# Decode attention beside a gMLP: the output weights of the gMLP laid out on other lanes

## The chip, the cores and the metric

The kernel runs on one core of one Trainium2 chip. A core has a matrix engine (PE, with its weight loads listed as PEld), a vector engine (DVE), a scalar engine (ACT), a general engine (POOL) and a sequencer for transfers (SP). Sixteen DMA engines carry data between the chip's main memory (DRAM) and the on-chip memory (SBUF), which has 128 lanes. The matrix engine writes to a smaller memory (PSUM). The metric is the device time of one execution in microseconds (us), as a median over runs.

## The reference

One decode step for four sequences, D = 640. The input x is normalised once. Attention uses 32 heads of 128 with caches of 4096 positions. A gMLP runs on the same normalised input, and both are added to x.

```python
xn = layernorm(x)                                   # x: 4 x 1 x 640
q = (xn @ wq) as 32 heads of 128                    # wq: 640 x 4096
p = softmax(q . k_cache / sqrt(128))                # caches: 4 x 32 x 4096 x 128
a = (p . v_cache) as 4096 columns @ wo              # wo: 4096 x 640
z = gelu(xn @ w_in)                                 # w_in: 640 x 1728
z1, z2 = z[:, :864], layernorm(z[:, 864:])
b = (z1 * (w_sp * z2 + b_sp)) @ w_out               # w_out: 864 x 640
out = x + a + b
```

All is bf16. The caches are 2 x 134 MB, so nearly all bytes moved are keys and values. w_out is 1.1 MB.

## The kernel before

The attention is cut into 16 tiles (8 heads of one sequence each). Each tile has 8 MB of keys and 8 MB of values, 64 KB to a lane. In the main loop DVE multiplies the keys by the spread query (product, L463), folds halves (fold, L477), PE sums the rest (sums, L489), DVE finishes the scores (row_sums, L500), and ACT takes the exponentials (L556). PE multiplies them with the values (weighted, L582) and the result is gathered (diag, L605) until the projection with wo at the end (group_proj, through add_out, L225).

SBUF has two slots for keys (pool kp) and one for values (pool vp), each 64 KB to a lane. A slot that holds other data is reused when its last reader is done. wq sits in the first key slot, the first keys in the second, and the second keys in the first one again, after wq. w_in and w_out sit together in the value slot (w_sb, L106 to L112), and the first values come after the gMLP has read them.

Work written before the `with tc.manual_schedule` block (L694) is put in order by a scheduler. Inside the block, PE, DVE, ACT and SP follow the order of the code. All large transfers are issued by SP, in one order: w_out's 128 lanes, wq, w_in, the rest of w_out, first keys, second keys, first values, and then keys and values in turn. An issue that has to wait holds up those behind it. The first two calls of load_k (L170, L308) stand before the block.

The gMLP (L331 to L435) multiplies w_in in 70 small matmuls (zT, L331), passes through a chain of short DVE and ACT steps, and ends in y, the gated product. w_out's rows 0 to 767 lie six to a lane on 128 lanes. The other 96 rows lie six to a lane on 16 lanes, filled by four transfers (L128) of four lanes each. Since y comes out of PE with 96 of its entries on 96 lanes, six selecting matmuls with columns of the identity (ye_ps, L423) turn them into 16 lanes of six, ACT copies them (L430), and add_out adds one product per row of a lane: 6 + 6 = 12 calls of four matmuls.

Of the kernel before, what the change touches and what calls it, by code (L numbers as in the profile page):

```python
# [17 lines left out]
def kernel(  # L18
# [14 lines left out]
    nc = tc.nc  # L33
    P = nc.NUM_PARTITIONS
    Bsz, Sq, D = A_x.shape
    _, H, S, Dh = A_k_cache.shape
    HD = A_wq.shape[1]
    F = B_w_in.shape[1]
    Fh = F // 2
    DC = D // P  # L40
# [13 lines left out]
    SLOT = NC * Dh  # L54
# [9 lines left out]
    WJ = WH * Dh // P  # L64
    WW = 2
    WR = NG * ROWS
    NFF = Fh // P
    TL = 16
    TK = (Fh - NFF * P) // TL
    TE = 4  # L70
    NFC = NFF + TK
    F0 = NFF * P
    TF = TL * TK
    NZ = NFF + 1
    assert F0 + TF == Fh and TF <= P
    NQ = 4
    NO = D // NQ
    REP = GW // Bsz
# [15 lines left out]
    def k_slot(name):  # L94
        return kp.tile([P, SLOT], BF16, tag="k", name=name)

    def v_slot(name):
# [7 lines left out]

    w_sb = v_slot("w_sb")  # L106
    w_in_sb = w_sb[:, 0 : DC * F].rearrange("p (c n) -> p c n", c=DC)
    w_out_sb = w_sb[:, DC * F : DC * F + NFC * D].rearrange("p (k n) -> p k n", k=NFC)
    y_at = DC * F + NFC * D
    y_rep = w_sb[:, y_at : y_at + (NZ + TK) * GW].rearrange(  # L110
        "p (k b r) -> p k b r", b=Bsz, r=REP
    )  # L112
    yT, yE = y_rep[:, 0:NZ], y_rep[:TL, NZ : NZ + TK]
    nc.sync.dma_start(
        out=w_out_sb[:, 0:NFF, :], in_=B_w_out[0 : NFF * P].rearrange("(p k) n -> p k n", k=NFF)
    )

    wq_t = k_slot("wq")[:, 0 : DC * HD].rearrange("p (c n) -> p c n", n=HD)
    nc.sync.dma_start(out=wq_t, in_=A_wq.rearrange("(p c) n -> p c n", c=DC))

    wsp_bf = const.tile([1, 1], BF16)
# [4 lines left out]
    nc.sync.dma_start(out=w_in_sb, in_=B_w_in.rearrange("(p c) n -> p c n", c=DC))  # L126
    for l in range(TL // TE):
        nc.sync.dma_start(  # L128
            out=w_out_sb[:TL, NFF:NFC, :].rearrange("(e l) k n -> e l (k n)", e=TE)[:, l],
            in_=B_w_out[F0:Fh].rearrange("(e l k) n -> e l (k n)", e=TE, k=TK)[:, l],  # L130
        )

    def kv_view(cache, i):
# [8 lines left out]
    def load_k(i):  # L142
        t = k_slot("k_nat")
        nc.sync.dma_start(out=t[:], in_=kv_view(A_k_cache, i))
        k_tiles[i] = t[:].rearrange("p (c d) -> p c d", d=Dh)
# [21 lines left out]
            for j0, j1 in zip(WO_CUTS[g], WO_CUTS[g][1:]):  # L167
                nc.sync.dma_start(out=t[:, g, j0:j1, :], in_=wo_v[g][:, j0:j1, :])

    load_k(0)  # L170


    ident = const.tile([P, P], BF16)
    make_identity(nc, ident[:])
    ident_f = const.tile([P, P], FP32)
    nc.gpsimd.tensor_copy(out=ident_f[:], in_=ident[:])
    eps_tile = const.tile([P, 1], FP32)
# [13 lines left out]
    for i in range(NSTAT):  # L191
# [9 lines left out]
        out=xn_bf,  # L201
# [21 lines left out]
    def add_out(lhsT, rhs, start=False, stop=False):  # L223
        for q in range(NQ):
            nc.tensor.matmul(  # L225
                out=out_ps[GW * q : GW * q + lhsT.shape[1], :],
                lhsT=lhsT,
                rhs=rhs[:, q * NO : (q + 1) * NO],
                start=start,
                stop=stop,  # L230
            )
# [73 lines left out]
            in_=qT_ps[:, :, :, :, 0],  # L305
        )

    load_k(1)  # L308


    GM = 2 * NZ * Bsz
    gm = {}
# [10 lines left out]
    def gmlp():  # L323
        zz, gw, gt, gz, sq = (gm[n] for n in ("zz", "gw", "gt", "gz", "sq"))
        zT = ps_pv.tile([P, 2, NZ, Bsz], FP32, tag="pv", name="zT")
        for t in range(2):
            f1 = t * Fh + F0
            w_t = w_in_sb[:, :, t * Fh : f1].rearrange("p c (f k) -> p c k f", k=NFF)
            for k in range(NZ):
                for c in range(DC):  # L330
                    nc.tensor.matmul(  # L331
                        out=zT[: P if k < NFF else TF, t, k, :],
                        lhsT=w_t[:, c, k, :] if k < NFF else w_in_sb[:, c, f1 : f1 + TF],
                        rhs=xnT[:, c, :],
                        start=(c == 0),
                        stop=(c == DC - 1),
                    )
        nc.vector.tensor_copy(out=zz[:, :, 0:NFF, :], in_=zT[:, :, 0:NFF, :])
        nc.vector.tensor_copy(out=zz[:TF, :, NFF:NZ, :], in_=zT[:TF, :, NFF:NZ, :])
        nc.vector.tensor_tensor(out=gw, in0=zz, in1=zz, op=ALU.mult)  # L340
        nc.vector.tensor_scalar(
            out=gw, in0=gw, scalar1=0.044715, scalar2=1.0, op0=ALU.mult, op1=ALU.add
        )
        nc.vector.tensor_tensor(out=gw, in0=gw, in1=zz, op=ALU.mult)
        nc.scalar.activation(
            out=gt, in_=gw, func=ACT.Tanh, scale=math.sqrt(2.0 / math.pi)
        )
        nc.vector.tensor_scalar(
            out=gt, in0=gt, scalar1=1.0, scalar2=0.5, op0=ALU.add, op1=ALU.mult
        )  # L350
        nc.vector.tensor_tensor(out=gz, in0=zz, in1=gt, op=ALU.mult)
        nc.vector.tensor_tensor(out=sq, in0=gz[:, 1, :, :], in1=gz[:, 1, :, :], op=ALU.mult)

        s_ps = ps_m.tile([1, 2, NZ, Bsz], FP32, tag="m", name="ln_ps")
        for n, src in enumerate((gz[:, 1, :, :], sq)):
            nc.tensor.matmul(
                out=s_ps[:, n, :, :], lhsT=ones_col[:], rhs=src, start=True, stop=True
            )
        st, ac = gm["st"], gm["ac"]
        mean_t = st[:, 0:Bsz]  # L360
        ex2_t = st[:, Bsz : 2 * Bsz]
        var_t = st[:, 2 * Bsz : 3 * Bsz]
        rst_t = st[:, 3 * Bsz : 4 * Bsz]
# [27 lines left out]
        nc.vector.tensor_tensor(out=tmp_t, in0=ac[:, 0:Bsz], in1=mean_t, op=ALU.mult)  # L391
        nc.vector.tensor_scalar(
            out=ac[:, Bsz : 2 * Bsz],
            in0=tmp_t,
            scalar1=-1.0,
            scalar2=bsp_t[:, 0:1],
            op0=ALU.mult,
            op1=ALU.add,
        )
        ac_ps = ps_m.tile([P, 2 * Bsz], FP32, tag="m", name="ac_ps")  # L400
        nc.tensor.matmul(
            out=ac_ps[:], lhsT=ones_row[:], rhs=ac[:], start=True, stop=True
        )
        ac_sb = work.tile([P, 2 * Bsz], FP32, name="ac_sb")
        nc.scalar.copy(out=ac_sb[:], in_=ac_ps[:])
        nc.vector.tensor_tensor(
            out=sq,
            in0=gz[:, 1, :, :],
            in1=ac_sb[:, None, 0:Bsz].to_broadcast([P, NZ, Bsz]),
            op=ALU.mult,  # L410
        )
        nc.vector.tensor_tensor(
            out=sq,
            in0=sq,
            in1=ac_sb[:, None, Bsz : 2 * Bsz].to_broadcast([P, NZ, Bsz]),
            op=ALU.add,
        )
        nc.vector.tensor_tensor(
            out=yT[:, :, :, 0], in0=gz[:, 0, :, :], in1=sq, op=ALU.mult
        )  # L420
        ye_ps = ps_m.tile([TL, TK, Bsz], FP32, tag="m", name="ye_ps")
        for k in range(TK):
            nc.tensor.matmul(  # L423
                out=ye_ps[:, k, :],
                lhsT=ident[:TF, :TF].rearrange("p (f k) -> p k f", k=TK)[:, k, :],
                rhs=yT[:TF, NFF, :, 0],
                start=True,
                stop=True,
            )
        nc.scalar.copy(out=yE[:, :, :, 0], in_=ye_ps[:])  # L430
        for k in range(NFC):
            if k < NFF:
                add_out(yT[:, k].rearrange("p b r -> p (b r)"), w_out_sb[:, k, :])
            else:
                add_out(yE[:, k - NFF].rearrange("p b r -> p (b r)"), w_out_sb[:TL, k, :])  # L435


    qbcs, scores, sums_ps, maxes, pms, pvs, es = {}, {}, {}, {}, {}, {}, {}
# [253 lines left out]

    E = mybir.EngineType
    with tc.manual_schedule(engines={E.PE, E.DVE, E.Activation, E.SP}):  # L694
        stage_q(0)
        gmlp()
        load_v(0, v_slot("v_nat"))
# [94 lines left out]
```

## Time and profile before

| | us |
|---|---|
| median of 3 runs | 661.47 |
| lowest and highest run | 661.35, 662.2 |
| the profiled execution | 661.68 |
| its span | 659.8 |
| busy in it: PE, PEld, DVE, ACT, POOL | 293.0, 127.5, 491.7, 35.1, 3.5 |
| granted clock of PE, mean | 0.715 of full |

The profile is of one execution. Its page gives busy time per engine, forty slices of the span, the DMA queues, and the chain of work that ended last. That chain follows each step back to whatever released it. Answers of the trace give the same execution instruction by instruction: start, length, engine, line, tile, and in brackets the idle time before it and what ended that. Times count from the start of the span. The 282.55 MB are moved at a mean of 428 GB/s. On SP, a line names the issue of a transfer and not its duration.

### The profile page before, as it was taken

How to read it: one execution, taken by the hardware profiler on the slowest of the kernel's cores; microseconds unless marked ns; L12 is line 12 of the kernel's file. 1: busy time of each engine (PE TensorE's matmuls, PEld its weight loads, DVE VectorE, ACT ScalarE, POOL GpSimd, SP SyncE). 2: the span in 40 equal slices, each digit the busy share in tenths (PEclk: the TensorE clock that was granted, in tenths of full speed). 3: DMA queues.
4: the chain of work that ended last, by engine and by line, in shares of the span. 5: the costliest groups of instructions: out<-in, count | busy, mean ns of one | idle time of the engine just before them, and what ended most of it. 6: DMA issues, size and time to landing. Idle time of an engine off the chain costs nothing.

```text
span 659.8 us, 4735 instructions
## 1 busy us (share of the span) xinstructions
PE 293.0 (44%) x2099; PEld 127.5 (19%) x2099; DVE 491.7 (75%) x222; ACT 35.1 (5%) x95; POOL 3.5 (1%) x18
## 2 busy tenths in 40 slices
PE   0513453535426163552626344362624516263646
PEld 0301121212112021210202112120311202031223
DVE  1249999959597795959779569986959599695851
ACT  0300000000000000000000000000000000000010
POOL 1000000000000000000000000000000000000000
PEclk9756687876758777675867757787775758768697
DMA  9999999999999999999999999999999999999996
GB/s 378 452 433 445 417 430 438 438 433 442 413 441 438 433 431 445 421 442 425 433 437 438 433 438 421 433 438 437 427 445 421 438 441 422 433 445 430 437 407 279
DMA packets 5700, 282.55 MB, mean 428 GB/s; under 512 B 668, under 2 KB 800, under 8 KB 1072
## 3 DMA queue, kind: packets, MB, share of 16 engines
q1 hardware_dynamic: 5658, 282.24, 98.9%
q8 instruction: 16, 0.26, 0.1%
q14 instruction: 4, 0.03, 0.0%
q10 hardware_dynamic: 22, 0.01, 0.0%
HBM read 282.24 MB, written 0.01 MB: 428 GB/s over the span
## 4 chain that ended last, share of the span: by engine, by line
DMA 49%; DVE 40%; PE 8%; issue 2%; ACT 1%; DVEq 0%; SPq 0%; ACTq 0%
DMA k_nat<-in_A_k_cache_dram 42%; DVE k_nat L463 24%; DVE k_nat L477 12%; DMA v_last<-in_A_v_cache_dram 6%; PE s_ps L489 6%; DVE s_sb L500 3%; PE pv L582 1%; ACT p L556 1%; DMA w_sb<-in_B_w_out_dram 1%; DVE m L509 1%; PE mT L514 0%; DVE nm L519 0%; PE out_ps L225 0%; PE o_ps L605 0%; PE den L622 0%
## 5 line engine op out<-in xcount | busy, mean ns | idle before, releaser
L463 DVE TENSOR_TENSOR k_nat<-k_nat,qbc 128x16384 bf16<-128x16384 bf16 x32 | 278.0, 8688 | 96.5 <-DMA k_nat<-in_A_k_cache_dram 96.5
L489 PE MATMUL s_ps<-k_nat,ident 128*128 128x512 bf16 x528 | 182.5, 523 | 140.3 <-DVE k_nat L477 140.3
L477 DVE TENSOR_TENSOR k_nat<-k_nat 128x8192 bf16<-128x8192 bf16 x31 | 136.7, 4409 | 0.0
L489 PEld LDWEIGHTS <-ident 128*128 128x128 bf16 x528 | 64.6, 128 | 247.6 <-DVE k_nat L477 124.5
L514 PE MATMUL mT<-ident_f,m 128*1 128x128 f32 x16 | 5.8, 360 | 160.0 <-DVE m L509 160.0
L582 PE MATMUL pv<-v_nat,pm 128*32 128x512 bf16 x960 | 56.1, 387 | 0.8 <-DVE pm L567 0.8
L500 DVE TENSOR_REDUCE s_sb<-s_ps 128x128 f32<-128x1024 f32 x32 | 39.0, 1218 | 3.8 <-PE s_ps L489 3.7
L582 PEld LDWEIGHTS <-pm 128*32 128x32 bf16 x1024 | 27.2, 101 | 36.1 <-issue 10.5
L514 PEld LDWEIGHTS mT<-ident_f,m 128*1 128x1 f32 x16 | 1.3, 79 | 167.8 <-DVE m L509 160.6
L567 DVE TENSOR_TENSOR pm<-p,own_c 128x2048 bf16<-128x2048 bf16 x16 | 19.6, 1225 | 15.3 <-ACT p L556 15.3
L556 ACT ACTIVATE p<-s_sb,nb 128x256 bf16<-128x256 f32 x16 | 8.1, 508 | 391.0 <-DVE nb_h L538 391.0
L605 PE MATMUL o_ps<-e,pick 128*32 128x128 f32 x128 | 17.0, 276 | 11.2 <-ACT e L592 11.2
L605 PEld LDWEIGHTS o_ps<-e,pick 128*32 128x32 f32 x128 | 12.7, 109 | 18.7 <-ACT e L592 18.7
L592 ACT COPY e<-pv 128x512 f32<-128x512 f32 x16 | 9.4, 586 | 70.4 <-PE pv L582 61.0
L530 PE MATMUL nb_ps<-nm,ones_row 1*128 1x8 f32 x32 | 9.1, 356 | 6.0 <-DVE nm L519 6.0
L301 DVE COPY qT<-qT_ps 128x64 bf16<-128x64 bf16 x2 | 0.4, 224 | 14.6 <-PE qT_ps L296 14.6
L519 DVE TENSOR_REDUCE nm<-mT 1x8 f32<-1x128 f32 x16 | 4.5, 279 | 7.3 <-PE mT L514 7.3
L530 PEld LDWEIGHTS nb_ps<-nm,ones_row 1*128 1x128 f32 x32 | 7.6, 293 | 10.5 <-DVE nm L519 9.8
L457 ACT CAST qbc<-qbc_ps 128x128 bf16<-128x128 f32 x16 | 4.3, 266 | 92.5 <-PE qbc_ps L449 92.5
L285 PE MATMUL q_ps<-wq,xnT_r 128*32 128x512 bf16 x40 | 3.8, 561 | 10.7 <-DMA wq<-in_A_wq_dram 10.7
L582 PE MATMUL pv<-v_last,pm 128*32 128x512 bf16 x64 | 6.0, 559 | 4.2 <-DMA v_last<-in_A_v_cache_dram 4.2
L622 PE MATMUL den<-ones_col,acc_h 128*32 128x1 f32 x8 | 1.0, 189 | 14.9 <-DVE acc_h L615 14.9
(95 smaller groups left out, 74.6 us busy)
## 6 DMA issues: line engine op xcount, KB each, us to landing
wq<-in_A_wq_dram SPq DMA_DIRECT2D x1, 5120.0 KB, 16.3
wo<-in_A_wo_dram SPq DMA_DIRECT2D x1, 2560.0 KB
w_sb<-in_B_w_in_dram SPq DMA_DIRECT2D x1, 2160.0 KB, 20.9
wo<-in_A_wo_dram SPq DMA_DIRECT2D x1, 1760.0 KB
w_sb<-in_B_w_out_dram SPq DMA_DIRECT2D x1, 960.0 KB
wo<-in_A_wo_dram SPq DMA_DIRECT2D x1, 640.0 KB, 25.0
k_nat<-in_A_k_cache_dram SPq DMA_DIRECT2D x16, 39.6
v_nat<-in_A_v_cache_dram SPq DMA_DIRECT2D x15, 33.3
```

The costliest lines, as they stand in the source:

```text
L463: nc.vector.tensor_tensor(out=part(i, u), in0=part(i, u), in1=qbcs[i][:, None, :].to_broadcast([P, UC, Dh]), op=ALU.mult,)
L477: nc.vector.tensor_tensor(out=t[:, :, 0:HD2], in0=t[:, :, 0:HD2], in1=t[:, :, HD2:Dh], op=ALU.add)
L489: nc.tensor.matmul(out=sums_ps[i][:, c : c + SC], lhsT=ident[:], rhs=t[:, c : c + SC, g * RW : (g + 1) * RW], start=(g == 0), stop=(g == n ...
L500: nc.vector.tensor_reduce(out=scores[i][:, u * UC : (u + 1) * UC], in_=sums_ps[i][:], axis=AX.X, op=ALU.add,)
L509: nc.vector.tensor_reduce(out=m1[:], in_=scores[i][:], axis=AX.X, op=ALU.max)
L514: nc.tensor.transpose(out=mT[:], in_=maxes[i][:], identity=ident_f[:])
L530: nc.tensor.matmul(out=nb_ps[:], lhsT=ones_row[:], rhs=maxes[i][:], start=True, stop=True)
L556: nc.scalar.activation(out=probs[i][:], in_=scores.pop(i)[:], func=ACT.Exp, bias=maxes.pop(i)[:], scale=scale_qk, accum_out=accs[hg][:, b ...
L567: nc.vector.tensor_tensor(out=pm[:], in0=probs.pop(i)[:] .rearrange("p (n c) -> p n c", c=CB)[:, :, None, :] .to_broadcast([P, NB, HT, CB] ...
L582: nc.tensor.matmul(out=pvs[i][j * GW : (j + 1) * GW, :], lhsT=pm[:, n, :, :].rearrange("p h c -> p (h c)"), rhs=v_nat[:, n * CB : (n + 1) ...
L592: nc.scalar.copy(out=es[i][:], in_=pvs.pop(i)[:].rearrange("p (c d) -> p c d", d=Dh))
L605: nc.tensor.matmul(out=o_ps[hg // NG][own_rows(hg), :], lhsT=pick[:, c, GW - HT - HT * b : 2 * GW - HT - HT * b], rhs=e[:, c, :], start=(b ...
```

## The change

w_out's rows 0 to 639 lie five to a lane on 128 lanes. The other 224 rows need 22.4 lanes of ten, so the last 240 rows (16 of them a second time) lie ten to a lane on 24 lanes. These lanes are no longer in w_sb but in the first key slot, behind wq. Four transfers of six lanes fill them, at the same place in SP's order. Each such lane has 12800 bytes, for 7680 before, and each of the 128 lanes of the large transfer 6400, for 7680.

The 224 entries of y now lie on 128 and 96 lanes, so the selection takes two matmuls for each of ten columns, summed in PSUM, with a selector that POOL writes at the end of w_sb: zeros, the identity, zeros. The 16 rows that are there twice are selected with zeros. add_out is called 5 + 10 = 15 times. zT has 70 matmuls as before.

The first key slot is now read until the end of the gMLP. The two first calls of load_k move into the ordered block, ahead of stage_q and gmlp, and the second one waits for the last add_out of the gMLP.

```diff
-    NFF = Fh // P
-    TL = 16
-    TK = (Fh - NFF * P) // TL
-    TE = 4
+    NFF = 5
+    TL = 24
+    TK = 10
+    TE = 6
...
-    NZ = NFF + 1
+    NZ = -(-Fh // P)
+    TF = Fh - (NZ - 1) * P
+    OV = TL * TK - (Fh - F0)
+    IL = P + OV
+    IW = (NZ - NFF - 1) * P + TL * TK
...
-    w_out_sb = w_sb[:, DC * F : DC * F + NFC * D].rearrange("p (k n) -> p k n", k=NFC)
-    y_at = DC * F + NFC * D
+    w_out_sb = w_sb[:, DC * F : DC * F + NFF * D].rearrange("p (k n) -> p k n", k=NFF)
+    y_at = DC * F + NFF * D
...
-    wq_t = k_slot("wq")[:, 0 : DC * HD].rearrange("p (c n) -> p c n", n=HD)
+    wq_sb = k_slot("wq")
+    wq_t = wq_sb[:, 0 : DC * HD].rearrange("p (c n) -> p c n", n=HD)
+    w_rest_sb = wq_sb[:TL, DC * HD : DC * HD + TK * D].rearrange("p (k n) -> p k n", k=TK)
...
     for l in range(TL // TE):
         nc.sync.dma_start(
-            out=w_out_sb[:TL, NFF:NFC, :].rearrange("(e l) k n -> e l (k n)", e=TE)[:, l],
-            in_=B_w_out[F0:Fh].rearrange("(e l k) n -> e l (k n)", e=TE, k=TK)[:, l],
+            out=w_rest_sb.rearrange("(e l) k n -> e l (k n)", e=TE)[:, l],
+            in_=B_w_out[Fh - TL * TK : Fh].rearrange("(e l k) n -> e l (k n)", e=TE, k=TK)[:, l],
         )
...
-    load_k(0)
...
+    sel = w_sb[:, SLOT - IW : SLOT]
+    nc.gpsimd.memset(sel[:, 0:IL], 0.0)
+    nc.gpsimd.tensor_copy(out=sel[:, IL : IL + P], in_=ident[:])
+    nc.gpsimd.memset(sel[:, IL + P : IW], 0.0)
...
-    load_k(1)
...
         for k in range(TK):
-            nc.tensor.matmul(
-                out=ye_ps[:, k, :],
-                lhsT=ident[:TF, :TF].rearrange("p (f k) -> p k f", k=TK)[:, k, :],
-                rhs=yT[:TF, NFF, :, 0],
-                start=True,
-                stop=True,
-            )
+            for w in range(2):
+                n = (P, TF)[w]
+                a = P * (1 - w) + k
+                nc.tensor.matmul(
+                    out=ye_ps[:, k, :],
+                    lhsT=sel[:n, a : a + TK * (TL - 1) + 1 : TK],
+                    rhs=yT[:n, NFF + w, :, 0],
+                    start=(w == 0),
+                    stop=(w == 1),
+                )
...
-                add_out(yE[:, k - NFF].rearrange("p b r -> p (b r)"), w_out_sb[:TL, k, :])
+                add_out(yE[:, k - NFF].rearrange("p b r -> p (b r)"), w_rest_sb[:, k - NFF, :])
...
     with tc.manual_schedule(engines={E.PE, E.DVE, E.Activation, E.SP}):
+        load_k(0)
+        load_k(1)
         stage_q(0)
         gmlp()
```

More of the change, by code (lines that the diff above doesn't have):

```diff
@@ L66 @@
     WR = NG * ROWS
-    NFF = Fh // P
-    TL = 16
-    TK = (Fh - NFF * P) // TL
-    TE = 4
+    NFF = 5
+    TL = 24
+    TK = 10
+    TE = 6
     NFC = NFF + TK
     F0 = NFF * P
-    TF = TL * TK
-    NZ = NFF + 1
-    assert F0 + TF == Fh and TF <= P
+    NZ = -(-Fh // P)
[3 more added lines that the diff above has]
+    IW = (NZ - NFF - 1) * P + TL * TK
+    assert NZ == NFF + 2 and 0 <= OV < P and IW >= IL + P
     NQ = 4
@@ L329, in gmlp @@
             for k in range(NZ):
+                a = (k - NFF) * P
+                n = TF if k == NZ - 1 else P
                 for c in range(DC):
                     nc.tensor.matmul(
-                        out=zT[: P if k < NFF else TF, t, k, :],
-                        lhsT=w_t[:, c, k, :] if k < NFF else w_in_sb[:, c, f1 : f1 + TF],
+                        out=zT[:n, t, k, :],
+                        lhsT=w_t[:, c, k, :]
+                        if k < NFF
+                        else w_in_sb[:, c, f1 + a : f1 + a + n],
                         rhs=xnT[:, c, :],
@@ L337, in gmlp @@
                     )
-        nc.vector.tensor_copy(out=zz[:, :, 0:NFF, :], in_=zT[:, :, 0:NFF, :])
-        nc.vector.tensor_copy(out=zz[:TF, :, NFF:NZ, :], in_=zT[:TF, :, NFF:NZ, :])
+        nc.vector.tensor_copy(out=zz[:, :, 0 : NZ - 1, :], in_=zT[:, :, 0 : NZ - 1, :])
+        nc.vector.tensor_copy(out=zz[:TF, :, NZ - 1, :], in_=zT[:TF, :, NZ - 1, :])
         nc.vector.tensor_tensor(out=gw, in0=zz, in1=zz, op=ALU.mult)
```

## The prediction

> **What bounds the kernel now.** I read the page's slices first, then the chain of work that ended last, then the order of SP's transfers, then the first 44 us in order of time.
>
> ```profile
> DMA  9999999999999999999999999999999999999996
> q1 hardware_dynamic: 5658, 282.24, 98.9%
> q8 instruction: 16, 0.26, 0.1%
> q14 instruction: 4, 0.03, 0.0%
> ```
>
> The DMA engines are busy in every slice up to the last. The small second row matters later: 16 fetches of instructions, 16 KB each, share the same engines.
>
> ```profile
> 138.45 40.70 DMA k_nat<-in_A_k_cache_dram
> ...
> 603.08 40.66 DMA v_last<-in_A_v_cache_dram
> 643.74 0.04 issue
> 643.78 6.03 PE pv L582 x64
> ```
>
> The chain (start, length, what) ends in the transfer v_last, which lands at 643.74. A fixed tail follows up to 659.8. So the time moves if v_last lands at another time, or if the tail changes.
>
> ```profile
> 6.03 15.70 SPq L144 DMA_DIRECT2D k_nat<-in_A_k_cache_dram  x2
> 35.88 0.33 SPq L150 DMA_DIRECT2D v_nat<-in_A_v_cache_dram  x1
> 76.47 0.33 SPq L144 DMA_DIRECT2D k_nat<-in_A_k_cache_dram  x1
> ```
>
> This is SP's order of issue: first keys at 6.03, second keys at 21.7 (the end of that line), first values at 35.88.
>
> ```profile
> 22.33 0.23 PE L449 MATMUL qbc_ps<-ident,q_l 128*128 128x128 bf16 x1
> 23.79 3.73 PE L331 MATMUL zT<-xnT_r,w_sb 128*128 128x4 bf16 x70 [1.23 <-DMA w_sb<-in_B_w_out_dram]
> 33.75 0.25 PE L423 MATMUL ye_ps<-w_sb,ident 96*16 96x4 bf16 x4 [1.10 <-DVE w_sb L418]
> 33.91 1.88 PE L225 MATMUL out_ps<-w_sb 128*32 128x160 bf16 x45
> 43.21 8.69 DVE L463 TENSOR_TENSOR k_nat<-k_nat,qbc 128x16384 bf16<-128x16384 bf16 x1 [9.60 <-DMA k_nat<-in_A_k_cache_dram]
> ```
>
> The gMLP runs from 23.79 to 35.8, while the first keys still arrive. It starts when the last small w_out transfer has landed.
>
> **The 16 streams.** The trace also keeps one record per transferred piece (start, duration, bytes). I joined each record to the one that starts where it ends, which gives 16 streams, one per DMA engine. A 64 KB piece takes 2.418 us, and no stream runs dry before v_last. The eighth 64 KB piece (the end of the first keys) ends at 41.70 to 41.98 on 11 streams. On four it ends at 42.82 to 43.11: these carried the 16 small w_out pieces, four each (4 x 0.291 = 1.16). On one it ends at 43.20, which had the first instruction fetch at 29.7. v_last ends at 640.78 to 642.27 on eight streams and at 643.50 to 643.82 on the other eight. Fifteen of the 16 KB fetches come before that. Each stops a stream for 0.80 to 0.95 and stretches its next piece by 0.47 to 0.55, some 1.4 us. They visit eight streams in turn, so seven carry two and one carries one. 640.85 + 2 x 1.4 = 643.65 is where seven end. The eighth late one is a small-piece stream that had two 8 KB fetches (0.30 + 0.53 each): 640.85 + 1.16 + 1.66 = 643.67. So instruction fetches decide which streams end last.
>
> **The change part by part.**
>
> *The large w_out transfer* has 6400 bytes to a lane for 7680, still eight pieces per stream. A 7680 piece takes 0.291 and a 5120 piece (the last wo transfers) 0.196, so 6400 is 0.243 between them. 8 x 0.048 = 0.38 us less on every stream.
>
> *The small transfers.* Now 24 lanes of 12800 bytes, in four transfers of six. Between 7680 (0.291) and 14080 (0.526), 12800 is 0.479. I take six streams with four pieces each, as four lanes gave four streams: 1.92 us. On the four old streams that is 1.92 - 1.16 - 0.38 = +0.38, on two new ones 1.92 - 0.38 = +1.54, on ten -0.38.
>
> [...]
>
> *Where v_last then ends.* Seven two-fetch streams: 643.5 to 643.82 less 0.38, at most 643.44. The stream with small pieces and two 8 KB fetches: 643.5 to 643.8 plus 0.38, so 643.9 to 644.2. The other three small-piece streams: at most 642.27 + 0.38 = 642.65. The two new ones, if they are without fetches of PE: 640.8 to 641.4 plus 1.54, at most 642.95. The last is 643.9 to 644.2 against 643.82: +0.1 to +0.4, and I take +0.25. Were that stream not last, it would be -0.38; both ends stay in the range.
>
> *Second keys behind the gMLP.* The room beside wq holds w_out rows until the last of add_out's matmuls (L225) reads them, so SP's second load_k, and the first load_v queued behind it, wait for that. In before only load_v did. Its time: zT no longer waits for the small transfers (another tile), only for w_in, whose last piece ends at 22.64, or 22.26 with the 0.38; then the matmul at 22.33 to 22.56 is the gate, so zT starts 1.2 earlier. The end of the gMLP had 6 + 24 + 24 matmuls in 2.04 us (33.75 to 35.79), 38 ns each; it gets 20 + 20 + 40 = 80, +1.0. Between 35.88 - 1.2 + 1.0 = 35.7 and, with no gain and twice the price, 37.9; I take 36. The first piece of a transfer starts 1.45 after its issue (0.73 to 2.18 at the start), so bytes come at 37.5 to 39.4. The earliest stream needs them at 41.70 - 0.38 = 41.3. Cost nothing; the cover is the rest of the first keys, 1.9 to 3.8 us. The third keys (issue 76.47, stream free at 80.4) had about as much, and no stream shows a gap there.
>
> *First keys land later.* Small-piece streams end them at 43.11 + 0.38 = 43.5 for 43.2, so DVE starts 0.3 later. DVE is without a break to 133 and then waits for keys from 138.45 to 179.14, which swallows it. The third keys' lead of 3.9 falls to 3.3, still over 1.45.
>
> *POOL* issues two memsets and a copy for the selector ahead of ident_f; by the pick memset (0.27) and the ident_f cast (0.28) some 0.8 us. The cover is PE's wait for wq up to 17.51, 10.5 us long. *PE* has 52 more instructions, so all but the first fetch come that much earlier in its program. The 15th (637.5) moves to about 631 and the 16th (654.5) to about 652, still after v_last: 15 remain. The tail is untouched.
>
> Sum: +0.25 (large transfer and small ones together), all else 0. On the profiled execution, 661.68 + 0.25 = 661.9; that execution lies 0.2 over the median of 661.47, so I say 661.7 for the median. A measurement of this kernel tells a change from none at about 0.2%, or 1.3 us; this is inside.
>
> **The rivals.**
>
> *The two new streams are among the eight that PE's fetches visit* (slower). They end at 643.6 - 0.38 + 1.92 = 645.1, up to 643.82 + 1.54 = 645.4: +1.5, 663.0. For it: eight of the 12 other streams have fetches, and no record says which numbers they have. [...] It decides as soon as one of the two has two fetches.
>
> *Six lanes go to two streams* (slower). 12 x 0.479 = 5.75 on each: 640.85 + 1.16 - 1.16 - 0.38 + 5.75 = 646.2, or 647.9 with two 8 KB fetches. +2.4 to +4.1, so 663.9 to 665.6. Against it: four lanes did make four streams.
>
> *The second keys come late* (slower). If they are issued after 39.85, all streams stand still for the difference. For it to reach 1.3 us the gMLP must end at 41.2, 5 us past my estimate; 2 us of standstill give 663.5.
>
> *The tail's clock falls otherwise* (faster). The granted clock is 0.59 over the 64 pv matmuls of the tail, and they take 6.03.
>
> ```profile
> 90.00:94.00 4.00, 4.00 (x66) 1.89 (x67) 4.00 (x1) 0.27 (x1) 0.00 (x0) 1.00 0.83 360
> 643.80:649.80 6.00, 6.00 (x66) 2.65 (x65) 0.00 (x0) 0.00 (x0) 0.00 (x0) 0.59 0.99 426
> ```
>
> (The columns are window, length, busy of PE, PEld, DVE, ACT and POOL, granted clock, DMA.) At a clock of 1.00 some 70 such matmuls took 4.0 us, so 64 would take 3.7: up to 2.4 us less. Half of it moved out would give 1.7 less with small gains of the streams, 659.8. For it: PE's program moves. Against it: its bursts hang on the keys' landings, which hardly move.
>
> **How the numbers follow.** The forecast has 0.53; new streams with fetches 0.20; two streams 0.06; late second keys 0.05; tail clock 0.16. The likeliest gives 661.7, its own range 661.0 to 662.3. For 8 in 10 I leave out two streams, late keys and the far half of the clock case: 660.0 to 663.3. Faster 0.16, same 0.53, slower 0.31.
>
> **What would show it.** Right: v_last lands within 0.4 of 643.74, four or six streams end the first keys last near 43.5, zT starts near 22.6, SP issues second keys and first values together near 36, and the slices stay at 9. Wrong: v_last at 645.2 or later (fetches on the new streams, or two streams), a slice under 9 near 40 us (late keys), or a pv group in the tail much shorter than 6.0.

## The result, and the profile after

The changed kernel takes 663.16 us (median of 12 executions, 662.55 to 663.77) beside 661.67 for the kernel before (12 executions): a ratio of 1.0019, 95% interval 1.0012 to 1.0027. It is slower by 1.5 us, about 0.2 per cent. The prediction of 661.7 was too low, and the time lies above the range of the forecast itself, 661.0 to 662.3; the first rival's 663.0 is what came.

The page of the changed kernel, its slices and queues (the profiled execution took 663.41 us, its span is 661.6):

```profile
DMA  8999999999999999999999999999999999999995
q1 hardware_dynamic: 5674, 282.26, 98.8%
q8 instruction: 16, 0.26, 0.1%
q14 instruction: 4, 0.03, 0.0%
```

The DMA engines are as full as before, and the number of PE's fetches (second small row) is the same 16. So no engine took over as the bound. The chain that ended last, from 600 us on (start, length, what):

```profile
604.26 41.47 DMA v_last<-in_A_v_cache_dram
645.72 0.04 issue
645.77 5.99 PE pv L594 x49
```

v_last lands at 645.72 where it landed at 643.74, and the first matmuls after it take 5.99 for 6.03: the whole difference arose before v_last landed, none of it in the tail. From the end of v_last's last 64 KB piece to the end of the span it is 16.38 for 16.39, and 16.2 to 16.6 in all the profiles here. SP's order of issue in the changed kernel:

```profile
5.89 29.69 SPq L149 DMA_DIRECT2D k_nat<-in_A_k_cache_dram  x2
35.69 0.37 SPq L155 DMA_DIRECT2D v_nat<-in_A_v_cache_dram  x1
75.76 0.33 SPq L149 DMA_DIRECT2D k_nat<-in_A_k_cache_dram  x1
```

The end of the first line is the second keys' issue, now at 35.58 with the first values right behind it. The first 44 us in order of time:

```profile
22.93 0.23 PE L461 MATMUL qbc_ps<-ident,q_l 128*128 128x128 bf16 x1
23.00 2.79 PE L338 MATMUL zT<-xnT_r,w_sb 128*128 128x4 bf16 x70
33.67 1.52 PE L232 MATMUL out_ps<-wq,w_sb 24*32 24x160 bf16 x40
43.27 8.69 DVE L475 TENSOR_TENSOR k_nat<-k_nat,qbc 128x16384 bf16<-128x16384 bf16 x1 [11.38 <-DMA k_nat<-in_A_k_cache_dram]
```

The gMLP starts right after the matmul of qbc and ends at 35.2. DVE starts on the first keys at 43.27, for 43.21: nothing here costs 1.5 us.

**The streams after.** The records of single pieces, joined into 16 streams as for the kernel before, show where it went. One thing first: the prediction counts the times of pieces from a fixed point, in the kernel before 0.43 us earlier than the start of the span, from which the page counts. Counted from the start of the span, the first large piece starts at 1.74 to 1.76 in every profile here, and v_last's last piece ends at 643.39 in the kernel before, not at 643.82. In the other executions the fixed point lies between 0.4 before and 0.2 after the start of the span, so by its count two executions differ by some tenths without cause. Below, all times count from the start of the span. The expectations keep the prediction's count.

The 24 small pieces of 12800 bytes took 0.479 each, on six streams with four each; the 6400-byte pieces took 0.244. Three streams without small pieces or fetches end v_last at 640.70 to 641.02, two with small pieces alone at 642.40 and 642.41, six with two of PE's fetches at 643.46 to 643.82, the one with small pieces and two 8 KB fetches at 643.86. One ends at **645.24**, 1.85 later than the last one before: it carried four small pieces and had two of PE's fetches, at 282.6 and 634.2. It is taken to be one of the two new streams, since in the profile of the kernel before none of the four with small pieces had such fetches. The other five with small pieces have none of PE's.

### The profile page after: what moved, and what is told of

Its sections match the earlier page's. It is cut to its first block, busy times and chain, and to the rows that moved or that the text cites. A ratio compares the mean times of both kernels' runs of the same rounds, so it can differ in the third digit from the quotient of the medians.

```text
span 661.6 us, 4786 instructions
## 1 busy us (share of the span) xinstructions
PE 296.0 (45%) x2125; PEld 128.7 (19%) x2125; DVE 491.7 (74%) x222; ACT 35.2 (5%) x95; POOL 4.2 (1%) x21
## 4 chain that ended last, share of the span: by engine, by line
DMA 49%; DVE 39%; PE 8%; issue 2%; ACT 1%; DVEq 0%; SPq 0%; ACTq 0%
DMA k_nat<-in_A_k_cache_dram 42%; DVE k_nat L475 24%; DVE k_nat L489 12%; DMA v_last<-in_A_v_cache_dram 6%; PE s_ps L501 6%; DVE s_sb L512 3%; PE pv L594 1%; ACT p L568 1%; DMA w_sb<-in_B_w_out_dram 1%; DVE m L521 1%; PE mT L526 0%; DVE nm L531 0%; PE out_ps L232 0%; PE o_ps L617 0%; PE den L634 0%
## 5 line engine op out<-in xcount | busy, mean ns | idle before, releaser
L308 DVE COPY qT<-qT_ps 128x64 bf16<-128x64 bf16 x2 | 0.4, 224 | 16.2 <-PE qT_ps L303 16.2
```

## The experiments

| run | what differs from the change | median us | ratio to before, 95% |
|---|---|---|---|
| after_again | nothing | 663.09 | 1.0022 (1.0013 to 1.0031) |
| e1_five | 25 lanes of nine, five to a transfer | 663.02 | 1.0020 (1.0012 to 1.0029) |
| e4_in_wq_slot | sizes of before, room and order of the change | 661.69 | 1.0000 (0.9992 to 1.0009) |
| e5_one_fetch_less | part of the score matmuls left out | 662.69 | 1.0011 (1.0002 to 1.0020) |
| e6_five_and_three | transfers of adjacent lanes | 666.15 | 1.0061 (1.0048 to 1.0073) |
| e7_all_streams | 32 lanes in one transfer | 663.16 | 1.0018 (1.0009 to 1.0027) |
| e8_few_fetches | part of the score and value matmuls left out | 662.08 | 1.0005 (0.9996 to 1.0014) |
| e9_before_few_fetches | the same cut in the kernel before | 661.45 | 0.9994 (0.9985 to 1.0003) |
| e10_five_by_four | 20 lanes of twelve, five to a transfer | 662.81 | 1.0015 (1.0006 to 1.0023) |
| e11_eight_by_four | 32 lanes of seven, eight to a transfer | 662.42 | 1.0012 (1.0003 to 1.0021) |
| e12_third_keys_early | part of the first tile's scores left out | 662.95 | 1.0020 (1.0012 to 1.0029) |
| e13_five_by_four_third_early | e10 with e12's cut | 662.01 | 1.0005 (0.9996 to 1.0014) |

The theory after the result: the sixth small-piece stream (the one that a transfer of six lanes loads and a transfer of five does not; the trace numbers no stream) is one of the eight that PE's fetches visit, and it alone makes the loss. Its rivals: the moved second keys, the sizes themselves, something else in the executions.

**The change again.**

> The changed kernel once more, beside the others. Theory of the streams (one of the two new streams of small pieces is also visited twice by PE's instruction fetches, and v_last waits for it): v_last lands near 645.4 again, 1.4 to 1.6 us over before (ratio 1.0022), with one stream some 1.4 us behind all others, and the pieces that were stretched between 160 and 210 us in the first profile need not come again. Theory of the stretched pieces (memory was slow for 0.5 us in that one execution, and that is part of the loss): without them the loss is about 1.0 us. Theory of the late keys (the second keys' wait for the gMLP costs): a gap in all streams near 41 us.

The time repeats: 663.09. In its profile (662.53, the lowest of its eleven) the streams can be told apart without doubt. Its latest three, and three late ones of the kernel before:

```
kernel        v_last ends  first keys end  small pieces  16 KB fetches before v_last  8 KB fetches
before        643.32       41.5            0             164.8, 516.3                 -
before        643.28       41.5            0             287.9, 637.0                 -
before        643.24       42.7            4             -                            107.9, 470.9
after_again   644.53       42.7            4             204.6, 553.8                 -
after_again   643.64       43.1            4             -                            105.9, 471.3
after_again   643.52       41.2            0             160.1, 514.1                 -
```

In the changed kernel a single stream has both small pieces and two fetches of PE, and it is last, 0.89 behind the next. In the kernel before such a stream would have ended at 640.42 + 1.16 + 2.8 = 644.4, and none ends after 643.39. The two rivals of the expectation do not show: no stream stands still near 41 us, and the pieces at 160 to 210 us are stretched by 1.1 in sum, for 8.4 in the first profile and 1.2 in the kernel before, while the median stays. The late stream ends 0.7 earlier than in the first profile, nearly all of it for fewer stretched pieces on it (1.2 in sum for 1.8).

The fetches' own lengths show which stream they visit. In the kernel before, the first turn took 961, 954, 880, 881, 941, 929, 921, 960 ns and the second 969, 951, 879, 881, 934, 933, 921. Two streams that follow each other in the turn are at about 0.88 nearly every time (one such fetch took 1.00 in after_again). This pair stands third and fourth here, seventh and eighth in the first profile of the change (886 and 886), fifth in after_again (878 and 879 for the late stream). The turn repeats within an execution, and the place of the pair in it differs from execution to execution, as if one turn began at another stream each time. The late stream is the first of the pair in both profiles of the change.

The chain that ended last is another one here than in the first profile:

```profile
631.05 25.64 DMA wo<-in_A_wo_dram
656.68 0.04 issue
656.73 0.69 PE out_ps L232 x20
```

The last part of wo follows v_last on the same streams. Its last piece ends 11.80 after v_last's last piece in every profile here, and in four of them (this one, e6, e8, e9) the execution ends with it. The tail thus has a second branch, also set by the streams: with 5.29 for the matmuls after v_last instead of 5.99, the time from v_last's last piece to the end is 16.20 instead of 16.38.

**The move alone: room, order and late second keys.**

```diff
-    w_out_sb = w_sb[:, DC * F : DC * F + NFC * D]...
+    w_rest_sb = wq_sb[:TL, DC * HD : DC * HD + TK * D]...   # as before: 16 lanes of 6 rows, 4 to a transfer
...
-    load_k(0)                  # ahead of the block
-    load_k(1)
...
     with tc.manual_schedule(...):
+        load_k(0)
+        load_k(1)
```

> The sizes of before (six rows a lane, 16 lanes, four transfers of four) with the small lanes in the room beside wq and the first two key loads in the ordered block, so that the second keys wait for the gMLP. Theory of the streams: no stream has more to carry than before, v_last near 643.8, no change (within 0.3 us). Theory of the late keys: all of the loss is here, +1.5 us.

The ratio is 1.0000. Second keys issued behind the gMLP cost nothing, and nothing is to be had by starting the gMLP on its own tile. Two lines of its timeline are worth keeping:

```profile
35.21 0.34 SPq L146 DMA_DIRECT2D k_nat<-in_A_k_cache_dram  x1
...
643.78 5.50 PE L578 MATMUL pv<-v_last,pm 128*32 128x512 bf16 x64 [2.22 <-DVE pm L563]
```

The tail's matmuls wait here for DVE's pm, which is ready at 643.74, and no longer for v_last, which is there by 643.7: with the streams as before, the two come at nearly the same time. The selector is not in this run; e13 below has it, the late second keys and larger pieces, and is 0.3 over the kernel before with all of them together.

**Five streams, 25 lanes.**

```diff
-    TL = 24
-    TK = 10
-    TE = 6
+    TL = 25
+    TK = 9
+    TE = 5
```

> 25 lanes of nine rows in five transfers of five lanes: five pieces of 11520 bytes (0.43 each, 2.16 in all) on five streams. Theory of the streams: if the visited stream is the sixth, no fetched stream carries small pieces; the two-fetch streams end v_last near 643.4 and the last is the small-piece stream with two 8 KB fetches, 643.67 - 0.38 - 1.16 + 2.16 = 644.3, so +0.5 us on before, 1.0 less than the change. If the visited one is the fifth: 645.4 + 0.24 = 645.65, +1.8 us. Theory of the late keys: as the change, +1.5, since the second keys wait all the same.

The time stayed at 663.02, which is neither number of the theory. It is near the number that the theory of the late keys gave, but no stream stands still near 41 us here, and e4 has the same wait at no cost. In its profile none of the five small-piece streams has a fetch of PE before v_last, so the theory held for the visits; but the pieces were slow. One stream's took 0.565, 0.848, 0.856 and 0.819 for 0.432, the first keys' pieces on all streams were stretched (6.8 us in sum, one piece by 1.6), and DVE started on the first keys at 45.01. In e1 the lanes of one transfer lie five apart; in the kernel before and in the change, where a piece took 0.291 and 0.479, they lie four apart. The suspicion that the place of the lanes slows the pieces led to e6, e7, e10 and e11.

**Fewer fetches.** Both leave part of the computation out, as their expectations say.

```diff
-            for g in range(n):
+            for g in range(n - 3 if i < NT - 2 else n):
...
-                    stop=(g == n - 1),
+                    stop=(g == (n - 3 if i < NT - 2 else n) - 1),
```

> The change, with five of the eight groups of columns summed in the scores of the first 14 tiles, so that PE has 336 instructions less (the scores of these tiles leave out three eighths of each key's products). PE is not what the transfers wait for. The 15th instruction fetch then comes after v_last instead of before it, and it is the one that visits the stream with small pieces for the second time. Theory of the streams: that stream ends at 645.4 - 1.4 = 644.0, level with the small-piece stream with two 8 KB fetches, and the time falls by 1.4 us, to +0.1 to +0.3 on before. Theories of the late keys and of the stretched pieces: as the change, +1.5 or +1.0.

The median fell by 0.4 and not by 1.4, but not evenly: two executions took 661.70 and 661.88, nine 662.57 to 663.18. The profiled one is the first of these: 13 fetches before v_last, the pair of short ones at the eighth and ninth place, so the sixth stream was visited once, ended at 643.37, and v_last landed at 643.82. With 13 fetches a stream escapes the second visit only if the turn reaches it sixth to eighth. That the other nine executions had another start of the turn is argued from the starts seen in the profiles; it was not seen.

```diff
 (as above, in the changed kernel and in the kernel before)
-        for n in range(c0 // CB, c1 // CB):
+        nb = 2 * CG if i < NT - 1 else NB
+        for n in range(nb):
...
-                stop=(n >= NB - CG),
+                stop=(n >= nb - CG),
```

> The change with much less work for PE: five of eight groups of columns summed in the scores of the first 14 tiles, and 8 of 64 blocks of the values multiplied in the first 15 tiles (the rest of both is left out). PE's program then has about 2000 instructions less, so that some seven instruction fetches come before v_last and no stream is visited twice, wherever the turn begins. The transfers of keys and values are the same. Theory of the streams: the visited small-piece stream ends at 640.5 + 1.92 + 1.4 = 643.8, and the last is the small-piece stream with two 8 KB fetches of another engine at 644.0: v_last lands 1.4 us earlier than in the change, and against the same cut of before the loss is 0.2 to 0.5 us instead of 1.45. Rival, that the small pieces, the selector or the second keys' wait cost the 1.45 by themselves: the loss against the same cut of before stays 1.4 to 1.5.

> The kernel before with the same work left out (five of eight groups in the scores of 14 tiles, 8 of 64 blocks of the values in 15 tiles), the control of the run before this one. Theory of the streams: with seven instruction fetches no stream is visited twice; the visited ones end near 642.3 and the last is the small-piece stream with two 8 KB fetches at 643.6 to 643.7, so v_last lands 0.1 to 0.2 earlier than in before and the time is -0.2 to 0.0. Rival that fetches by PE don't matter: no change in the streams' spread.

With seven fetches before v_last, none visits a stream twice. The changed kernel is then at 662.08 and the kernel before at 661.45, measured on the same chip: 0.63 apart for 1.43 to 1.49 without the cut. The two chains end alike, first e8 and then e9:

```profile
627.13 28.75 DMA wo<-in_A_wo_dram
655.88 0.04 issue
```

```profile
626.81 28.42 DMA wo<-in_A_wo_dram
655.22 0.04 issue
```

v_last's last piece ends at 643.75 and 643.09, 0.66 apart, in both kernels on the stream with small pieces and two 8 KB fetches. The visited small-piece stream ends at 643.52 in e8; with two visits in the change it ended at 645.24. So over half of the change's loss goes with the second visits. The medians alone would leave that loose, since the interval of each is some 0.6 wide to either side; the streams show it. The 0.66 left is more than the 0.2 to 0.5 expected: 0.38 is the larger small pieces less the saving on the large transfer, as worked out, and some 0.25 is more stretched pieces on that stream in e8 (1.33 in sum for 1.08).

**Which lanes a transfer fills.**

```diff
-    TL = 24
-    TK = 10
-    TE = 6
+    TL = 32
+    TK = 7
+    TE = 32                    # one transfer
```

> The change with the 224 rows on 32 lanes of seven, in one transfer that all 16 streams share, two pieces of 8960 bytes (0.34) each. Theory of the streams: every stream has 0.68 more and 0.38 less; the two-fetch streams end at 643.8 + 0.3 = 644.1, the stream with two 8 KB fetches at 643.67 - 1.16 + 0.3 = 642.8. v_last lands 0.3 later than in before and about 1.2 earlier than in the change: +0.3 on before. Rival, that the second keys' wait or the selector costs the loss: as the change, +1.45.

```diff
-    for l in range(TL // TE):
+    cuts = (0, 5, 10, 15, 18, 21, 24)
+    for l0, l1 in zip(cuts, cuts[1:]):
...
-            out=w_rest_sb.rearrange("(e l) k n -> e l (k n)", e=TE)[:, l],
+            out=w_rest_sb[l0:l1].rearrange("l k n -> l (k n)"),
```

> The change with its 24 lanes filled by three transfers of five lanes and three of three, so that three streams have six pieces, two have three, and the sixth stream none. Theory of the streams, with the visited one sixth: two-fetch streams end near 643.4; a stream with six pieces and no fetch at 640.85 - 0.38 + 2.87 = 643.3, with one 8 KB fetch at 643.8; the one with two 8 KB fetches at 643.6 if it has three pieces and 645.0 if it has six. So between -0.1 and +0.3 on before if it has three, +1.2 if six. If the visited stream is the fifth instead: 643.6 - 0.38 + 1.44 = 644.7 to 644.9, +1.0.

Both theories missed, e6 by 3 us or more. The 663.16 of e7 is what its rival gave, but e4 and e13 leave no 1.4 us for the second keys' wait and the selector, and the traces show another cause. The timeline of e7 where DVE starts on the first keys:

```profile
45.06 8.69 DVE L475 TENSOR_TENSOR k_nat<-k_nat,qbc 128x16384 bf16<-128x16384 bf16 x1 [13.15 <-DMA k_nat<-in_A_k_cache_dram]
```

The same line of e6:

```profile
48.28 8.69 DVE L476 TENSOR_TENSOR k_nat<-k_nat,qbc 128x16384 bf16<-128x16384 bf16 x1 [16.30 <-DMA k_nat<-in_A_k_cache_dram]
```

The first keys land 1.8 and 5.0 later than with the change. DVE waits for them that much longer. In e7, whose one transfer fills 32 adjacent lanes, the 8960-byte pieces took 0.62 on average and up to 0.79, for 0.338 in e11 below. In e6, whose transfers fill five or three adjacent lanes each, 12800-byte pieces took up to 1.53, for 0.479 in the change, and the pieces of the first keys that ran beside them were stretched by 33 us in sum over the 16 streams (10.5 in e7, 0.1 in e11 below). In e6 the third keys then came late too: they were issued at 81.95, and nine streams stood still near 82 us, for 8.1 in sum.

**The same counts with the lanes of a transfer four apart.**

```diff
-    TL = 24                    |    TL = 24
-    TK = 10                    |    TK = 10
-    TE = 6                     |    TE = 6
+    TL = 20                    |    TL = 32
+    TK = 12                    |    TK = 7
+    TE = 5     # e10           |    TE = 8     # e11
```

> As the change, but 32 lanes of seven rows (224 rows) in four transfers of eight lanes: eight streams carry four pieces of 8960 bytes each, and each of the eight fills four neighbouring lanes. The lanes and the pieces are those of the one transfer on all 16 streams, where two streams shared four neighbouring lanes and a piece took 0.48 to 0.79. Theory (the sharing of neighbouring lanes was what slowed that run): pieces at 0.338, 1.35 on each of the eight, the first keys' pieces not stretched; streams six to eight are visited twice and end last, at 643.6 to 643.8 less 0.38 plus 1.35, so 644.6 to 644.8: +0.8 to +1.0 on the kernel before, 662.4 to 662.7, below the change. Rival (many streams at once are what slows the pieces, whatever the lanes): pieces at 0.5 to 0.8 again, 2 to 3.2 on each, v_last at 645.3 or later, 663.2 or more.

> As the change, but 20 lanes of twelve rows (240 rows, as many as the change) in four transfers of five lanes, so that five streams carry four pieces of 15360 bytes each, and each of the five fills four lanes that lie side by side (in the run with 25 lanes each filled five). Estimate of a piece, between 14080 bytes (0.526) and 17280 (0.644): 0.573, so 2.29 on each of the five. Theory (PE's fetches visit the sixth stream and not the first five; neighbouring lanes written by several streams at once are what slowed the run with 25 lanes): pieces take 0.57, the first keys' pieces are not stretched, no small-piece stream has a 16 KB fetch before v_last, the stream with two 8 KB fetches ends at 643.67 - 1.16 - 0.38 + 2.29 = 644.4 and is the last: +0.6 on the kernel before, 662.2 to 662.4. Rival A (the order of the lanes is not what slowed that run, five streams as such are): pieces at up to 0.85 and stretched keys again, 663.0 as there. Rival B (one of the five is visited): 643.6 - 0.38 + 2.29 = 645.5, 663.3 or more.

Which lanes a stream fills is the author's count from the order of the rows; the trace names no lane of a piece. What the kernels fix is where the lanes of one transfer lie: four apart in both. In e11 all 32 pieces took 0.338, and the time fell to 662.42; in e10 below the 20 pieces took 0.573. Five streams had slow pieces where the lanes of a transfer lie five apart (e1, up to 0.856 for 0.432) or side by side (e6, up to 1.53 for 0.479): slow pieces go with the place of the lanes here, not with the number of streams. The streams of e11 are the cleanest picture of the visits:

```
v_last ends  first keys end  small pieces  16 KB fetches before v_last (length, ns)
644.25       42.5            4             245.4 (879), 596.9 (879)
644.14       42.4            4             206.6 (886), 555.8 (878)
643.13       41.3            0             164.6, 513.7
643.09       41.3            0             116.2, 475.0
```

Two of the eight small-piece streams are visited, not three as the expectation had it, and these two are the pair with the short fetches. They end 1.0 to 1.3 after the two-fetch streams without small pieces, which is the 1.35 of four pieces. The chain:

```profile
604.53 40.17 DMA v_last<-in_A_v_cache_dram
644.71 0.04 issue
644.75 6.56 PE pv L594 x49
```

In e10 the 20 pieces took 0.573, as estimated, and the first keys' pieces were hardly stretched beside them (0.03 in sum). Yet its profiled execution took 663.45 and the median of 662.81 is above the theory's 662.2 to 662.4. Windows of e10 around 80 us (window, length, busy of PE, PEld, DVE, ACT and POOL, clock, DMA share, GB/s; a piece counts whole where it starts, so a share can pass 1):

```profile
76.00:80.00 4.00, 1.79 (x6) 0.46 (x4) 4.00 (x2) 0.00 (x0) 0.00 (x0) 0.85 0.87 377
80.00:84.00 4.00, 0.93 (x3) 0.57 (x3) 3.50 (x4) 0.00 (x0) 0.00 (x0) 0.58 0.93 360
```

The same windows of the change:

```profile
76.00:80.00 4.00, 0.00 (x0) 0.00 (x0) 4.00 (x2) 0.00 (x0) 0.00 (x0) 1.00 1.02 442
80.00:84.00 4.00, 0.93 (x3) 0.57 (x3) 3.50 (x4) 0.00 (x0) 0.00 (x0) 0.57 1.10 475
```

Here the DMA engines did run dry in e10, too briefly for the page's slices of 16 us. The cause is one step earlier, in e10's timeline of PE and SP:

```profile
71.19 6.59 PE L501 MATMUL s_ps<-k_nat,ident 128*128 128x512 bf16 x16 [8.92 <-DVE k_nat L489]
77.82 0.33 SPq L149 DMA_DIRECT2D k_nat<-in_A_k_cache_dram  x1
```

The third keys wait for the last 16 score matmuls of the first tile. Those took 6.59 (5.18 in the change's profile) after a DVE that had started at 43.92 (43.27). The keys were issued at 77.82, and the streams came free from 79.69 on. Two of them started on the new keys without a gap, at 80.07 and 80.12; the seven others that were free by 80.2 stood still for 0.7 to 2.2 us and started at 80.87 to 81.89, up to 4.1 us after the issue. Gaps (9.5) and stretched pieces when the streams started close together (6.6) make some 16 us over the streams, 1.0 on each. The last stream, one of the seven, ended at 645.27; the stream with two 8 KB fetches, which had no gap, at 644.21. An estimate: without the standstill that stream would have been last, at 644.2 or somewhat earlier, and the execution at most 663.45 - 1.06 = 662.4, the upper end of the theory's range.

**The third keys early.** The edit, in the change and in e10 (the tile's scores have two parts, not the four that the expectation names):

```diff
         n = (HD2 if folded(i, u) else Dh) // RW
+        n = 2 if i == 0 and u == NC // UC - 1 else n
```

> As the change, but the last of the four parts of the first tile's scores sums two of its eight column groups only (the output is then not the reference's): 4 matmuls of s_ps for 16, so that SP issues the third keys some 3.5 us earlier, at 72 to 73 instead of 75.76 and 76.45. PE's program gets 24 instructions shorter, a tenth of the way between two fetches. Theory (the visited sixth stream is the change's loss): the third keys had lead enough, the time stays at 662.9 to 663.3. Rival (in a good part of the executions the third keys' first pieces come after the streams are free near 79.9, as in the run with 20 lanes, where they were issued at 77.82 and all streams stood still for 0.6 to 1.2): 662.7 or less.

> The kernel with 20 lanes of twelve rows in transfers of five, with the same cut in the last part of the first tile's scores (the output is then not the reference's): the third keys are issued at 73 to 74.5 instead of 77.82. Theory (what held that run above its 662.2 to 662.4 was the standstill of all streams at 80 us, some 1.0 in its profiled execution and less in others): no gap between the pieces at 80 us, five streams end the first keys last and none of them has a 16 KB fetch before v_last, the stream with two 8 KB fetches ends last at 644.2 to 644.5, 662.2 to 662.5. Rival (one of the five is visited in part of the executions): 662.8 again.

In the change the early keys (72.79) leave the time at 662.95, inside the theory's range: their lead was enough or nearly so. In the five-stream kernel (73.14) the gap is gone and the time falls by 0.8 to 662.01, ratio 1.0005, slightly below the range expected. Its last stream is the one with two 8 KB fetches (644.52), the streams with two of PE's fetches end at 643.70 at the latest, and the short pair (879, 878) visits none of the five:

```profile
604.12 40.73 DMA v_last<-in_A_v_cache_dram
644.85 0.04 issue
644.89 5.96 PE pv L595 x64
```

e12 and e13 were measured on one chip and move the same 240 rows, over six streams and over five. The sixth stream is worth 662.95 - 662.01 = 0.94 of the loss; some 0.3 is left for all the rest of the change, the larger pieces on five streams among it. None of the kernels that compute everything beats the one before.

## Why the prediction was wrong

**The step that failed** is the second half of "where v_last then ends": "the two new ones, if they are without fetches of PE", at most 642.95, so that the stream with two 8 KB fetches would be last. One of the two is visited twice. The "if" had only the four small-piece streams without visits in the kernel before to go by, four of sixteen; with transfers of five lanes none was visited either (e13), with six one was (after_again, e12) and with eight two (e11). By the prediction's own count eight of the 12 other streams are visited; if nothing else were known, both new ones would be quiet with a chance of 4/12 x 3/11, about 0.1, while the visited case was given 0.20. The wide range, to 663.3, held the result only because this rival was in it.

The rival's own sum was right in mechanism and near in size: 645.1 to 645.4 for that stream, which is 644.7 to 645.0 from the start of the span, measured 645.24 and, in after_again, 644.53; and 663.0, measured 663.16. After_again, e11, and e12 against e13 show the cause.

**The sum of the rest** was near: the stream with small pieces and two 8 KB fetches was put at 643.9 to 644.2 (643.5 to 643.8 from the start of the span) and ended at 643.86 and 643.64. e13, where such a stream is last, is 0.3 over the kernel before.

**The two counts of time** in the prediction touch one of its terms: 1.45 from issue to first piece takes the issue from one count and the piece from the other. In one count it is 1.75 - 0.73 = 1.02.

**The large transfer:** 6400 bytes took 0.244 for the 0.243 worked out. That streams without small pieces end earlier for it shows in after_again: the first of them ends the first keys at 40.92 for 41.27 in the kernel before, and those without fetches end v_last at 639.88 to 640.50 for 640.35 to 640.61. It does not show in the first profile (640.70 to 641.02), where each stream's pieces were stretched by some 0.5 in sum at 160 to 210 us. Why, no run shows.

**The small transfers:** 0.479 to a piece, four to each of six streams, to the digit. That six lanes go to six streams the prediction took from four on four; five and eight lanes gave five and eight streams in e10 and e11. One transfer of 32 lanes, put at +0.3 in e7's expectation, came out at +1.4, with slow pieces (0.62 on average for 0.338).

**Second keys** cost nothing, as said (e4, ratio 1.0000), and were issued at 35.24 for 36. zT started at 23.00 (22.6 was said), since qbc's matmul came at 22.93 in that execution; in after_again it started at 22.29. The four or six latest ends of the first keys were foreseen near 43.5 (43.1 from the start of the span); they were at 42.66 to 42.90.

**The third keys' lead** was called safe against 1.45 us from issue to first piece, a number from the start of the kernel. At 80 us it did not hold: in e10 the streams had their first pieces 2.2 to 4.1 after the issue, and a lead of 79.69 - 77.82 = 1.9 was too short. It is not a fixed number either: in e6 it was 0.9 to 1.6 for the streams that stood still, and in e1 a lead of 2.4 left no gap. In the change's first profile the lead is 79.86 - 75.76 = 4.1. In after_again it is 79.59 - 76.45 = 3.1, and the pieces at 80 us were stretched by 2.1 in sum, 0.1 to a stream; in e8 it was 79.39 - 76.71 = 2.7, and the streams lost 0.8 in gaps and 2.6 in stretched pieces, 0.2 each. So this cover was nearly used up in some executions, while the prediction took it to be twice what was needed.

**The tail's clock:** the 64 pv matmuls after v_last took 5.3 to 6.6 over the profiles of these kernels (e6's left aside), 6.03 in the kernel before (granted clock 0.59) and 5.99 (0.60) and 5.29 in the change's two. It moves from execution to execution, not with the change. The prediction gave 0.16 to a faster tail, worth up to 2.4 us. It overlooked the branch through wo: in the kernel before, wo's last piece ends at 655.19, and from v_last's last piece to the end it is 16.20 to 16.36 in the executions that end with wo, for 16.39 here: an estimate from these is that a faster tail could have gained at most 0.2.

## What to carry to other kernels

When 16 DMA streams bound a kernel, add up every stream by itself: steady pieces, extra pieces, and the instruction fetches that happen to land on it. Transfers of four, five, six and eight rows loaded as many streams here (before, e10, the change, e11), and the four such transfers of a kernel loaded the same ones (four pieces each in the kernel before, the change and e11). So the price of such a load depends on whether the last stream it reaches is already a late one: the same 240 rows cost 0.3 us on five streams and 1.25 on six (e13, e12). An "if" about such a stream belongs in the sum with the weight of what the records leave open, and the lead of each refill wants its issue-to-first-piece time from the same stretch of the trace. And before two executions are compared to some tenths of a microsecond, all times have to count from the same start.

## What the hardware showed that was not expected

**Adjacent lanes.** Small pieces ran slower where one transfer fills lanes that lie side by side: 0.62 on average for 0.338 in e7, with 32 lanes to the transfer, and up to 1.53 for 0.479 in e6, with five and three. With lanes five apart they were slower too (e1, up to 0.856 for 0.432). The first keys' pieces that ran beside them were stretched, by 33 us in sum over the 16 streams in e6 and 10.5 in e7. With the lanes of a transfer four apart, pieces of 7680, 8960, 12800 and 15360 bytes took 0.291, 0.338, 0.479 and 0.573, on four, eight, six and five streams (before, e11, the change, e10). The kernel with transfers of adjacent lanes took 3 us longer than the change (e6, 666.15 for 663.16). What in the chip makes the place of the lanes count, no run here shows.

**The turn of the fetches.** In the profiles with 13 to 15 fetches before v_last, PE's fetches visit eight of 16 streams in a turn. The trace does not number the streams, but the small pieces mark some of them: with transfers of four and five lanes none of these was visited (before, e10, e13), with six one, the first of the pair of short fetches (after, after_again, e12), and with eight two, the pair itself (e11). That fits, without showing it, transfers that fill the streams in one order, and one fixed turn that begins at another place each time: the pair of short fetches stood first and second in e4's profile, second and third in e10's, third and fourth in the kernel before, fifth and sixth in e13's, seventh and eighth in the change's first. With 15 fetches before v_last only a stream that comes eighth escapes the second visit. That would make a part of the spread between executions; it was seen in profiles only, one execution at a time.
